# One shared block of rows for the real zeroth frequency of both batches in a Fourier and two-MoE kernel

## The chip, the cores and the metric

The kernel runs on one core of one Trainium2 chip. Time is device time in microseconds (us) for one execution of the whole program; a run reports the median of several. The engines are PE (TensorE, matrix products; PEld is its weight load), ACT (ScalarE), DVE (VectorE), POOL (GpSimd) and SP (SyncE, which here issues nearly all DMAs, one after the other). A line such as L737 is a line of the kernel as printed below.

## The reference, cut to what matters

Three layers follow one another. Only the first is touched.

```python
X = np.fft.rfft(x, axis=1)                       # x: 2 batches, 3008 positions, 256 channels
Yr = Xr @ w_r - Xi @ w_i + b_r                   # frequency mixing, 256 x 256
Yi = Xr @ w_i + Xi @ w_r + b_i
Yr, Yi = shrink(Yr), shrink(Yi)                  # sign(y) * max(|y| - 0.01, 0)
y = np.fft.irfft(Yr + 1j * Yi, n=3008, axis=1)
h = y @ w_in;  y = (h * cos(h)) @ w_out          # first MoE layer, 256 -> 2048 -> 256
h = y @ w_in2; y = (h * relu6(h + 3) / 6) @ w_out2
```

## The kernel before, in words

The transform of 3008 points is split as 47 x 64. The **first transform** (`a_part`, L562) works along the 47; of its output frequencies only k2 = 0 to 23 are made, each with a cosine row and a minus-sine row, for 64 positions n2. Its result is kept as a rounded part `zh` and a rest `zl`, with the layout (channel, pair p of two k2, half kc of the channels, four rows of 64: two per k2). For k2 = 0 the sine row is zero throughout. Batch 1's results wait in `z1` and are moved into `zh` and `zl` by `stage` (ACT and POOL) when batch 0 no longer needs the place.

For each of 12 pairs p of each of 2 batches, **mixing** (`w_mm`, L662) makes two blocks of 128 rows (two rows x 64 positions) and 512 columns (w_r and w_i), six matmuls each, and `w_split` cuts each into a rounded part and a rest (ACT, DVE). The **second transform** along the 64 (`b_mm`, L691) starts from a PSUM tile filled with the bias (`fill`) and adds six matmuls of 512 columns: two frequencies of 256 channels. `shrink_a`, `shrink_b`, `shrink_hi` and `shrink_lo` apply the threshold and split again. The **inverse** along the 64 (`v_mm`, L730) is three matmuls of 512 columns; `v_store` copies the result out of PSUM (ACT, L735) and writes it to `u_dram` in memory (SP, L737, two DMAs). Later `load_u` reads `u_dram` back with a table (L410 and L412), and `y_mm` (L421) does the inverse along the 47.

`k2_step(i)` runs these as a pipeline, 24 steps and a drain: in step i the mixing is of pair i, the second transform of pair i-1, the shrink of pair i-2, and the inverse and the store of pair i-3, all counted through both batches (so step 15 stores pair 0 of batch 1). While batch 0 is mixed, steps 0 to 7 also hold batch 1's first transform, whose data come through a ring of three buffers (`x_ring`, L542). Steps 17 to 22 (`Y_EARLY`) also hold the first six groups of `y_mm`; `load_u` of groups 0 to 3 is called at the ends of steps 14 to 17. In the same steps `cv.step` converts the MoE weights from 64-bit floats, with loads and stores of its own on SP. The order on PE, ACT and SP is the order of the program text here, and SP issues nothing behind an entry that waits. After the steps the MoE layers run, nearly all on PE.

The order inside a step that the argument needs:

```python
w_mm(b, 2 * p)                 # PE
fill(*now)                     # ACT or DVE
y_mm(...)                      # PE, steps 17 to 22
shrink_a(*late); w_split(b, 2 * p); a_part(a, 0); v_mm(*last)
shrink_hi(*late); v_store(*last); w_mm(b, 2 * p + 1)
w_split(b, 2 * p + 1); a_part(a, 1); stage(k); b_mm(*now)
```

Of the kernel before, what the change touches and what calls it, by code (L numbers as in the profile page):

```python
# [9 lines left out]
F32 = mybir.dt.float32  # L10
F32R = mybir.dt.float32r
# [3 lines left out]
AF = mybir.ActivationFunctionType  # L15
ALU = mybir.AluOpType
# [4 lines left out]
N1, N2, NSEQ = 47, 64, 3008  # L21
NB, D, DFF = 2, 256, 2048
# [29 lines left out]
Y_EARLY = range(17, 23)  # L52
FILL_DVE = range(13, 22)
LEAD = 6
OPERANDS = (1, 2, 2, 2, 2, 3)
SEVEN = (0, 2, 4, 6)
V11, V12, V22, V1, V2, V3, V4 = range(7)
# [25 lines left out]
def _tables():  # L83
    n1 = np.arange(N1)
    k2 = np.arange(NK2)
    ta = np.zeros((2, 48, NPAIR, NK2, 2))
    tg = np.zeros((2, NK2, 2, NPAIR, 2, N1))
    for i in range(NPAIR):
        for s in range(2):
            n = 64 * n1 + 2 * i + s  # L90
            c, sn = _trig(np.outer(n, k2), NSEQ)
            ta[s, :N1, i, :, 0] = c
            ta[s, :N1, i, :, 1] = -sn
            w = np.where(k2 == 0, 1.0, 2.0)[:, None] / NSEQ
            tg[s, :, 0, i, s, :] = w * c.T
            tg[s, :, 1, i, s, :] = -w * sn.T
    j = np.arange(N2)
    c, s = _trig(np.outer(j, j), N2)
    sg = np.where(j < N2 // 2, 1.0, -1.0)[None, :]
    f1 = np.zeros((2, N2, 2, N2))  # L100
    f1[0, :, 0], f1[1, :, 0] = c, s
    f1[0, :, 1], f1[1, :, 1] = -s, c
    f2 = np.zeros((2, N2, 2, N2))
    f2[0, :, 0], f2[1, :, 0] = sg * s, -sg * c
    f2[0, :, 1], f2[1, :, 1] = sg * c, sg * s
    g = np.zeros((2, N2, 2, 2, NPAIR))
    cc = c.reshape(N2, NPAIR, 2).transpose(0, 2, 1)
    ss = s.reshape(N2, NPAIR, 2).transpose(0, 2, 1)
    for z in range(2):
        g[0, :, z, 0], g[1, :, z, 0] = cc[:, z], -ss[:, z]  # L110
        g[0, :, z, 1], g[1, :, z, 1] = ss[:, z], cc[:, z]
    parts = []
    for m in (-f1, -f2, -g):
        parts += _split(m.reshape(128, 128))

    fg = np.concatenate(parts, axis=1)
    ta_rows = np.zeros((112, NPAIR * DOF))
    ta_rows[:48], ta_rows[64:] = ta.reshape(2, 48, -1)
    return (
        ta_rows.reshape(112, 4, NPAIR * 12).transpose(1, 0, 2).astype(np.float32),  # L120
        tg.reshape(ROWS, NPAIR * TP).astype(np.float32),
        np.ascontiguousarray(fg, dtype=np.float32),
    )
# [3 lines left out]
def fourier_moe_moe_kernel(ctx, tc, x, w_r, w_i, b_r, b_i, ta, tg, fg, win1, wout1, win2, wout2, out):  # L127
# [3 lines left out]
    def f32(ap):  # L131
        return ap.bitcast(F32)
# [43 lines left out]
    def pool_sub(out, x, y):  # L176
        nc.gpsimd.tensor_tensor(out, x, y, op=ALU.subtract)  # L177
# [339 lines left out]
    with ExitStack() as actx:  # L517
        apool = actx.enter_context(tc.tile_pool(name="apool", bufs=1))
        with tc.manual_schedule(engines={mybir.EngineType.PE, mybir.EngineType.SP, mybir.EngineType.Activation}):
# [54 lines left out]

            def stage(q):

                act.activation(zh[:, q], z1[:, q], AF.Copy)
                pool_sub(zl[:, q], z1[:, q], f32(zh[:, q]))

            def zero(engine, at):  # L580
                engine.memset(at, 0.0)
# [45 lines left out]
                    sp.dma_start(wst[:, k, z], w[k * 128 : (k + 1) * 128])  # L627

            def late_loads2():
                sp.dma_start(fg_raw, fg)  # L630
                for z, src in enumerate((b_r, b_i)):
                    sp.dma_start(bias[64 * z : 64 * z + 64, 0], src.partition_broadcast(64))

            def late_loads3():
                cv.add(0, range(4))

            def constants(k):
                if k < 2:
# [10 lines left out]

            def w_mm(b, k2, parts=range(2), terms=range(3)):  # L650
                p = k2 // 2
                if k2 % 2 == 0 and 0 in parts and 0 in terms:
                    ph_t[b, p] = [
                        apool.tile([128, 2, 2, D], F32R, tag=f"ph{z}", bufs=2, name=f"ph{z}_{b}_{p}") for z in range(2)
                    ]
                if 0 in parts and 0 in terms:
                    pp_t[b, k2] = h_bank(f"pp{b}_{k2}").rearrange("p (a e) -> p a e", a=2)
                pp = pp_t[b, k2]
                for kc in parts:
                    for n in terms:  # L660
                        za, wb = ((zh, wh), (zl, wh), (zh, wl))[n]
                        pe.matmul(  # L662
                            pp.rearrange("p a e -> p (a e)"),
                            lhsT=za[:, p, kc, 2 * (k2 % 2) : 2 * (k2 % 2) + 2, :].rearrange("p r n -> p (r n)"),
                            rhs=wb[:, kc, :],
                            start=(kc == 0 and n == 0),
                            stop=(kc == 1 and n == 2),
                        )

            def w_split(b, k2):  # L670
                ph, pl = (t[:, k2 % 2] for t in ph_t[b, k2 // 2])
                pp = pp_t.pop((b, k2))
                act.activation(ph, pp, AF.Copy)
                dve.tensor_tensor(pl, pp, f32(ph), op=ALU.subtract)

            def fill(b, p):

                bp_t[b, p] = bp = psum.tile([128, 2, D], F32, tag="acc0", bufs=2, name=f"bp{b}_{p}")
                rows = bias.to_broadcast([128, 2, D])
                if b * NP + p in FILL_DVE:  # L680
                    dve.tensor_copy(bp, rows)
                else:
                    act.activation(bp, rows, AF.Copy)

            def b_mm(b, p):
                bp = bp_t[b, p]
                ph, pl = ph_t.pop((b, p))
                n = 0
                for m in range(2):
                    for fi, src in ((2 * m, ph), (2 * m, pl), (2 * m + 1, ph)):  # L690
                        pe.matmul(bp, lhsT=fgr[:, fi, :], rhs=src[:, :, m, :], start=False, stop=(n == 5), skip_group_check=True)  # L691
                        n += 1

            def shrink_a(b, p):

                u_t[b, p] = persist.tile([128, 2, D], F32, tag="r", bufs=5, name=f"u{b}_{p}")
                act.activation(u_t[b, p], bp_t[b, p], AF.Relu, bias=-LAM, scale=1.0)

            def shrink_b(b, p):
                bp, u = bp_t[b, p], u_t.pop((b, p))  # L700
                dve.scalar_tensor_tensor(bp, bp, LAM, u, op0=ALU.add, op1=ALU.min)

            def shrink_sb(b, p):
# [5 lines left out]
            def shrink_hi(b, p, copy=None):  # L709
                sh = persist.tile([128, 2, D], F32R, tag="gh", bufs=4, name=f"sh{b}_{p}")  # L710
                sl = persist.tile([128, 2, D], F32R, tag="gl", bufs=5, name=f"sl{b}_{p}")
                if copy:
                    copy(sh, bp_t[b, p])
                else:
                    act.activation(sh, bp_t[b, p], AF.Copy)
                sh_t[b, p] = (sh, sl)

            def shrink_lo(b, p):
                sh, sl = sh_t[b, p]
                dve.tensor_tensor(sl, bp_t.pop((b, p)), f32(sh), op=ALU.subtract)  # L720

            def shrink_lo_sb(b, p):
                sh, sl = sh_t[b, p]
# [2 lines left out]
            def v_mm(b, p):  # L726
                vp = psum.tile([128, 2, D], F32, tag="acc1", bufs=2, name=f"vp{b}_{p}")
                sh, sl = sh_t.pop((b, p))
                for n, (fi, src) in enumerate(((4, sh), (5, sh), (4, sl))):
                    pe.matmul(vp, lhsT=fgr[:, fi, :], rhs=src, start=(n == 0), stop=(n == 2))  # L730
                vp_t[b, p] = vp

            def v_store(b, p):
                v = persist.tile([128, 2, D], F32, tag="o", bufs=4, name=f"v{b}_{p}")
                act.activation(v, vp_t.pop((b, p)), AF.Copy)  # L735
                for s in range(2):
                    sp.dma_start(  # L737
                        u_dram[b][s, 4 * p : 4 * p + 4].rearrange("(k r) i e -> (r i) k e", r=2),
                        v[64 * s : 64 * s + 64],
                    )  # L740

            def k2_step(i):
                now, late, last = (divmod(i - k, NP) for k in range(1, 4))
# [2 lines left out]
                more = i < NB * NP  # L746
                a, q = NA + i, STAGED[i : i + 2]
                if i == 0:
                    for n in range(3):
                        w_mm(0, 0, (0,), (n,))  # L750
                        w_mm(0, 1, (0,), (n,))
                    w_mm(0, 0, (1,))
                elif more:
                    w_mm(b, 2 * p)
                if i >= 1:
# [4 lines left out]
                if i >= 2:  # L760
                    shrink_a(*late)
                    cv.step(rate[0])
                    shrink_b(*late)
                w_split(b, 2 * p)
                for g, ec in early:
                    y_out(g, ec)
                if a < 2 * NA:
# [54 lines left out]
            for i in range(NB * NP):  # L822
                k2_step(i)
                if i == 0:
                    constants(2)
                if Y_EARLY[0] - 3 <= i <= Y_EARLY[0]:
                    load_u(i - Y_EARLY[0] + 3)
                if i == NB * NP - len(OPERANDS):
                    ready = operands(0)
                if i >= NB * NP - len(OPERANDS):  # L830
                    for _ in range(OPERANDS[i - NB * NP]):
                        next(ready, None)
# [544 lines left out]
```

## Time and profile before

| | |
|---|---|
| time, median of 3 runs (lowest to highest) | 1142.51 us (1142.24 to 1143.01) |
| the profiled execution's own time | 1142.83 us |
| its span, first to last instruction | 1140.8 us |
| PE busy | 1134.2 us, 99% |
| DVE, ACT, POOL busy | 78%, 75%, 76% |
| granted TensorE clock, mean | 0.999 |

The span is one execution recorded by the profiler; 2.0 us of the execution's own time lie outside it. Matmuls are pipelined, so a matmul's own length (389 ns at 512 columns) is longer than the distance from one start to the next. Where a row says "[0.40 <-PE pp L662]", the engine sat idle 0.40 us before the row and the work named released it. A landing time counts from the issue of the DMA.

### The profile page before, as it was taken

How to read it: one execution, taken by the hardware profiler on the slowest of the kernel's cores; microseconds unless marked ns; L12 is line 12 of the kernel's file. 1: busy time of each engine (PE TensorE's matmuls, PEld its weight loads, DVE VectorE, ACT ScalarE, POOL GpSimd, SP SyncE). 2: the span in 40 equal slices, each digit the busy share in tenths (PEclk: the TensorE clock that was granted, in tenths of full speed). 3: DMA queues.
4: the chain of work that ended last, by engine and by line, in shares of the span. 5: the costliest groups of instructions: out<-in, count | busy, mean ns of one | idle time of the engine just before them, and what ended most of it. 6: DMA issues, size and time to landing. Idle time of an engine off the chain costs nothing.

```text
span 1140.8 us, 16407 instructions
## 1 busy us (share of the span) xinstructions
PE 1134.2 (99%) x5285; PEld 950.3 (83%) x5285; DVE 888.7 (78%) x1302; ACT 851.0 (75%) x1627; POOL 864.1 (76%) x709
## 2 busy tenths in 40 slices
PE   9999999999999999999999999999999999999998
PEld 7888887888888887888889988888888888888897
DVE  5888876776888979887888777677787877867775
ACT  4788788777888888888888876666676676667664
POOL 3556747975997897887987987787878878777854
PEclk9999999999999999999999999999999999999999
DMA  9645968434113114012215520241231222221300
GB/s 224 192 141 173 273 183 287 153 120 154 65 59 105 36 65 139 19 60 98 75 56 193 231 94 33 65 139 32 65 107 44 90 71 64 74 94 32 100 3 33
DMA packets 73925, 120.99 MB, mean 106 GB/s; under 512 B 7904, under 2 KB 47504, under 8 KB 73328
## 3 DMA queue, kind: packets, MB, share of 16 engines
q1 hardware_dynamic: 73712, 119.80, 33.2%
q8 instruction: 42, 0.69, 0.3%
q14 instruction: 43, 0.35, 0.1%
q10 hardware_dynamic: 128, 0.15, 0.0%
HBM read 78.11 MB, written 41.81 MB: 105 GB/s over the span
## 4 chain that ended last, share of the span: by engine, by line
PE 94%; DMA 2%; DVE 1%; POOL 1%; ACT 1%; issue 1%; SPq 0%; POOLq 0%; ACTq 0%; DVEq 0%
PE acc L909 38%; PE hb L909 17%; PE ha L909 11%; PE pp L662 6%; PE hd L909 6%; PE hc L909 5%; PE part L909 5%; PE bp L691 3%; PE yp L421 2%; PE vp L730 1%; DMA x_big<-in_x_dram 1%; PE zp L562 1%; POOL gl L177 1%; DMA wst<-in_w_i_dram 1%; DVE sums L941 0%
## 5 line engine op out<-in xcount | busy, mean ns | idle before, releaser
L177 POOL TENSOR_TENSOR gl<-r,gh 128x512 fp32r<-128x512 f32 (+1 forms) x322 | 424.4, 1335 | 119.7 <-ACT gh L897 109.3
L909 PE MATMUL acc<-gh,wo 128*128 128x512 f32 (+1 forms) x1276 | 445.5, 386 | 0.0
L909 PEld LDWEIGHTS acc<-gh,wo 128*128 128x128 f32 x1276 | 239.6, 188 | 44.3
L909 PE MATMUL acc<-gl,wo 128*128 128x512 f32 (+1 forms) x638 | 246.1, 386 | 0.5 <-POOL gl L177 0.5
L909 PE MATMUL hb<-tok,wi 128*128 128x512 f32 (+1 forms) x864 | 242.1, 388 | 0.1
L897 ACT ACTIVATE gh<-r 128x512 fp32r<-128x512 f32 (+1 forms) x344 | 205.3, 617 | 4.9 <-DVE r L872 4.3
L909 PEld LDWEIGHTS hb<-tok,wi 128*128 128x128 f32 x864 | 160.1, 188 | 34.1 <-DVE hd L921 3.6
L883 ACT ACTIVATE r<-r 128x512 f32<-128x512 f32 (+1 forms) x192 | 118.7, 618 | 56.7 <-DVE r L870 56.7
L909 PE MATMUL ha<-tok,wi 128*128 128x512 f32 (+1 forms) x576 | 159.7, 385 | 0.0
L177 POOL TENSOR_TENSOR sums_lo<-sums,sums_hi 128x512 fp32r<-128x512 f32 (+1 forms) x80 | 100.7, 1277 | 62.4 <-ACT sums_hi L988 40.2
L909 PEld LDWEIGHTS acc<-gl,wo 128*128 128x128 f32 x638 | 119.8, 188 | 23.6 <-POOL gl L177 1.5
L909 PEld LDWEIGHTS ha<-tok,wi 128*128 128x128 f32 x576 | 108.0, 188 | 20.6 <-ACT yo L440 0.2
L1174 ACT ACTIVATE p<-hc 128x512 f32<-128x512 f32 (+1 forms) x96 | 56.4, 588 | 78.2 <-PE hc L909 78.0
L921 DVE TENSOR_TENSOR hd<-p,hb 128x512 f32<-128x512 f32 (+1 forms) x96 | 65.6, 683 | 62.2 <-ACT p L1174 36.3
L474 POOL TENSOR_TENSOR tok<-st,tok 128x512 fp32r<-128x512 f32 (+1 forms) x81 | 103.3, 1289 | 3.4 <-ACT tok L477 3.4
L909 PE MATMUL hc<-tok,wi 128*128 128x512 f32 (+1 forms) x288 | 80.3, 387 | 0.0
L909 PE MATMUL hd<-tok,wi 128*128 128x512 f32 (+1 forms) x288 | 79.9, 386 | 0.0
L1149 ACT ACTIVATE hb<-ha 128x512 f32<-128x512 f32 (+1 forms) x96 | 55.2, 575 | 25.8 <-PE ha L909 25.3
L921 DVE TENSOR_TENSOR hc<-p,hb 128x512 f32<-128x512 f32 (+1 forms) x96 | 65.3, 680 | 11.1 <-PE hb L909 10.2
L909 PEld LDWEIGHTS hc<-tok,wi 128*128 128x128 f32 x288 | 53.7, 188 | 11.4 <-DVE r L887 1.6
L909 PEld LDWEIGHTS hd<-tok,wi 128*128 128x128 f32 x288 | 54.1, 188 | 10.3
L474 POOL TENSOR_TENSOR st<-st 128x512 f32<-128x512 f32 (+1 forms) x44 | 56.7, 1288 | 1.2
(197 smaller groups left out, 2121.3 us busy)
## 6 DMA issues: line engine op xcount, KB each, us to landing
wo<-ws_dram SPq DMA_DIRECT2D x50, 256.0 KB, 3.2
st<-x_dram SPq DMA_DIRECT2D x18, 512.0 KB, 5.5
rawi<-in_win_dram SPq DMA_DIRECT2D x16, 512.0 KB, 4.1
rawo<-in_wout_dram SPq DMA_DIRECT2D x16, 512.0 KB, 3.8
wi<-wi_dram SPq DMA_DIRECT2D x4, 1792.0 KB, 8.5
u_dram<-v SPq DMA_DIRECT2D x48, 128.0 KB, 2.4
u_sb<-u_dram SPq DMA_DIRECT2D x16, 384.0 KB, 4.1
wo<-wo_dram SPq DMA_DIRECT2D x10, 512.0 KB, 6.5
```

The costliest lines, as they stand in the source:

```text
L177: nc.gpsimd.tensor_tensor(out, x, y, op=ALU.subtract)
L421: pe.matmul(yp[:, i * TP : (i + 1) * TP], lhsT=u_sb[g][:, i, ec * 128 : (ec + 1) * 128], rhs=tg_sb[g][:, i * TP : (i + 1) * TP], start=Tru ...
L474: (dve if jj == NJ + 1 and not ringed else nc.gpsimd).tensor_tensor(out, x, y, op=op)
L562: pe.matmul(zp[:, i * ROWS : (i + 1) * ROWS].rearrange("p (s f) -> p s f", s=2), lhsT=xt[:rows, i, kc * 128 : (kc + 1) * 128], rhs=tt[:row ...
L662: pe.matmul(pp.rearrange("p a e -> p (a e)"), lhsT=za[:, p, kc, 2 * (k2 % 2) : 2 * (k2 % 2) + 2, :].rearrange("p r n -> p (r n)"), rhs=wb[ ...
L691: pe.matmul(bp, lhsT=fgr[:, fi, :], rhs=src[:, :, m, :], start=False, stop=(n == 5), skip_group_check=True)
L883: act.activation(r, r, AF.Sin, bias=math.pi / 2, scale=1.0)
L897: act.activation(gh[:, :n], self.r[:, :n], AF.Copy)
L909: pe.matmul(h[:, :n], lhsT=w, rhs=x, start=start and j == 0, stop=stop and j == 2, skip_group_check=True)
L921: dve.tensor_tensor(h[:, :n], r[:, :n], x[:, :n], op=ALU.add)
L1149: act.activation(b[:, :n], a[:, :n], AF.Copy)
L1174: act.activation(p5[:, :n], c[:, :n], AF.Copy)
```

## The change

Both batches' zeroth frequency is real, so the second row of k2 = 0 is free. The table `ta` now has the cosine in both rows, `stage` moves only the second row of batch 1's pair 0, and so the block of pair 0, k2 = 0 of batch 1 holds batch 0 in its first 64 rows and batch 1 in its last 64. Batch 0 mixes no block for k2 = 0, and its pair 0 runs in `fill`, `b_mm`, `shrink_*`, `v_mm` and `v_store` on one frequency (256 columns). Pair 0 of batch 1 uses other tables and another bias for k2 = 0, 33 real and 31 imaginary rows per batch, so its second transform and inverse run as two sets of matmuls of 256 columns. Its `v_store` writes the zeroth rows of both batches. The new tables and the bias rows are loaded by `late_loads4` at the end of step 1 (seven DMAs on SP, two of which fill the unused sine rows of `u_dram`) and rounded by `zero_tables` (ACT) in steps 2 to 4. `load_u(0)` moves from the end of step 14 to the end of step 15, with `load_u(1)` behind it; `y_mm` stays where it was.

```diff
@@ _tables @@
             ta[s, :N1, i, :, 1] = -sn
+            ta[s, :N1, i, 0, 1] = c[:, 0]
...
+    half = NPAIR + 1
...
+    for b in range(2):
+        fz1[b, :, b, :half], fz1[b, :, b, half:] = c[:, :half], -s[:, 1:NPAIR]
+        fz2[b, :, b, :half], fz2[b, :, b, half:] = s[:, :half], c[:, 1:NPAIR]
+        gz[b, :half, :, b] = np.where(j[:half] % NPAIR, 2.0, 1.0)[:, None, None] * cc[:half]
+        gz[b, half:, :, b] = -2.0 * ss[1:NPAIR]
...
@@ stage @@
-                act.activation(zh[:, q], z1[:, q], AF.Copy)
-                pool_sub(zl[:, q], z1[:, q], f32(zh[:, q]))
+                hi, lo, z = (t[:, q, :, q == 0 :] for t in (zh, zl, z1))
+                act.activation(hi, z, AF.Copy)
+                pool_sub(lo, z, f32(hi))
...
+            def late_loads4():
+                t = persist.tile([128, 2048], F32, tag="st", bufs=1, name="zero_k2_raw")
+                zero_k2.append(persist.tile([128, 8, 128], F32R, tag="u_sb", name="zero_k2"))
+                zero_k2.extend((t[:, 768:1024], t))
+                sp.dma_start(t[:, :768], fg[:, 768:])
+                for b in range(NB):
+                    for src, o0, o1 in ((b_r, 0, NPAIR + 1), (b_i, NPAIR + 1, N2)):
+                        sp.dma_start(t[64 * b + o0 : 64 * b + o1, 768:1024], src.partition_broadcast(o1 - o0))
+                    sp.dma_start(u_dram[b][:, 1], fg[0:64, 0:D].rearrange("(s i) e -> s i e", s=2))
+
+            def zero_tables(n):
+                act.activation(zero_k2[0][:, 2 * n : 2 * n + 2].rearrange("p a b -> p (a b)"), zero_k2[2][:, 256 * n : 256 * n + 256], AF.Copy)
+
+            def columns(b, p):
+                return slice((b, p) == (0, 0), 2)
+
+            def tables(b, p):
+                if (b, p) == (1, 0):
+                    return ((slice(0, 1), zero_k2[0]), (slice(1, 2), fgr))
+                return ((columns(b, p), fgr),)
...
@@ fill @@
+                elif (b, p) == (1, 0):
+                    act.activation(bp[:, 0], zero_k2[1], AF.Copy, scale=-1.0)
+                    act.activation(bp[:, 1], bias[:, 0], AF.Copy)
                 else:
-                    act.activation(bp, rows, AF.Copy)
+                    act.activation(bp[:, columns(b, p)], rows[:, columns(b, p)], AF.Copy)
...
@@ b_mm (v_mm and the shrink functions are cut to columns and tables alike) @@
+                for cs, tab in tables(b, p):
+                    n = 0
+                    for m in range(2):
+                        for fi, src in ((2 * m, ph), (2 * m, pl), (2 * m + 1, ph)):
+                            pe.matmul(bp[:, cs], lhsT=tab[:, fi, :], rhs=src[:, cs, m, :], start=False, stop=(n == 5), skip_group_check=True)
+                            n += 1
...
@@ v_store @@
+                    if p:
+                        sp.dma_start(
+                            u_dram[b][s, 4 * p : 4 * p + 4].rearrange("(k r) i e -> (r i) k e", r=2),
+                            v[64 * s : 64 * s + 64],
+                        )
+                        continue
+                    sp.dma_start(u_dram[b][s, 2:4].rearrange("r i e -> (r i) e"), v[64 * s : 64 * s + 64, 1])
+                    for r in range(NB * b):
+                        sp.dma_start(u_dram[r][s, 0], v[64 * s + 32 * r : 64 * s + 32 * r + 32, 0])
@@ k2_step @@
                 if i == 0:
-                    for n in range(3):
-                        w_mm(0, 0, (0,), (n,))
-                        w_mm(0, 1, (0,), (n,))
-                    w_mm(0, 0, (1,))
+                    banks[0] += 1
+                    w_mm(0, 1, (0,))
...
-                w_split(b, 2 * p)
+                if i:
+                    w_split(b, 2 * p)
...
@@ the loop over the steps @@
-                if Y_EARLY[0] - 3 <= i <= Y_EARLY[0]:
-                    load_u(i - Y_EARLY[0] + 3)
+                if i == LOAD_ZERO:
+                    late_loads4()
+                if LOAD_ZERO < i < LOAD_ZERO + 4:
+                    zero_tables(i - LOAD_ZERO - 1)
+                for g in {NP + 3: (0, 1), NP + 4: (2,), NP + 5: (3,)}.get(i, ()):
+                    load_u(g)

```

## Rows read from the trace of the kernel before

**Rows 1.** The page: the chain that ended last, by engine.

```profile
PE 94%; DMA 2%; DVE 1%; POOL 1%; ACT 1%; issue 1%; SPq 0%; POOLq 0%; ACTq 0%; DVEq 0%
```

**Rows 2.** Who PE waited for, whole span: total us, times, longest us.

```profile
PE zp L562 <- DVE zl L573: 0.8, 3, 0.3
PE acc L909 <- POOL gl L177: 0.5, 2, 0.3
```

**Rows 3.** Timeline of PE in step 0: start us, us, work, count.

```profile
21.57 0.71 PE L662 MATMUL pp<-wh,zh 128*128 128x512 f32 x2
...
23.75 0.50 PE L662 MATMUL pp<-wh,zl 128*128 128x512 f32 x1
...
24.32 1.03 PE L562 MATMUL zp<-ta_ring,x_ring 96*128 96x96 f32 x8
25.14 0.48 PE L662 MATMUL pp<-wh,zh 128*128 128x512 f32 x1
```

**Rows 4.** The ring's first load: SP's timeline, and DMA issues with landing us.

```profile
17.89 0.34 SPq L542 DMA_DIRECT2D x_ring<-in_x_dram  x1
...
x_ring<-in_x_dram SPq DMA_DIRECT2D x1, 384.0 KB, 5.7
```

**Rows 5.** Timeline of PE in the first MoE layer, 512 and 448 columns.

```profile
333.44 0.84 PE L909 MATMUL ha<-tok,wi 128*128 128x512 f32 x3
334.12 0.39 PE L909 MATMUL acc<-gh,wo 128*128 128x512 f32 x1
...
627.14 0.77 PE L909 MATMUL ha<-tok,wi 128*128 128x448 f32 x3
627.75 0.36 PE L909 MATMUL acc<-gh,wo 128*128 128x448 f32 x1
```

**Rows 6.** Timeline of SP, steps 1 and 2.

```profile
32.40 0.58 SPq L542 DMA_DIRECT2D x_ring<-in_x_dram  x1
37.69 0.39 SPq L203 DMA_DIRECT2D rawo<-in_wout_dram  x1
```

**Rows 7.** Timeline of PE at the first early group of the last inverse.

```profile
116.09 1.92 PE L421 MATMUL yp<-tg_sb,u_sb 96*128 96x94 f32 x16
```

**Rows 8.** Timeline of ACT, steps 9 to 15.

```profile
82.14 0.42 ACT L302 ACTIVATE whii011h<-w 128x256 fp32r<-128x256 f32 x1
...
84.89 0.60 ACT L673 ACTIVATE ph<-pp 128x512 fp32r<-128x512 f32 x1 [0.40 <-PE pp L662]
...
104.61 0.59 ACT L735 ACTIVATE v<-vp 128x512 f32<-128x512 f32 x1
...
109.14 0.59 ACT L735 ACTIVATE v<-vp 128x512 f32<-128x512 f32 x1
```

**Rows 9.** Busy time in a stretch: PE, PEld, DVE, ACT, POOL, clock, DMA.

```profile
98.50:115.00 16.50, 16.50 (x75) 13.66 (x74) 16.21 (x24) 12.27 (x24) 11.38 (x9) 1.00 0.62 184
```

**Rows 10.** Timeline of SP, steps 14 to 16.

```profile
105.23 1.23 SPq L737 DMA_DIRECT2D u_dram<-v  x2
108.46 0.33 SPq L410 DMA_DIRECT2D u_sb<-u_dram  x1
108.86 1.24 SPq L412 DMA_DIRECT2D tg_sb<-in_tg_dram  x1
...
111.47 0.59 SPq L274 DMA_DIRECT2D wo_dram<-whio011h  x1
```

**Rows 11.** DMA issues of steps 14 to 17: count, KB, landing us.

```profile
u_dram<-v SPq DMA_DIRECT2D x2, 128.0 KB, 2.4
...
u_dram<-v SPq DMA_DIRECT2D x2, 128.0 KB, 3.1
...
u_sb<-u_dram SPq DMA_DIRECT2D x1, 384.0 KB, 3.9
...
u_sb<-u_dram SPq DMA_DIRECT2D x1, 384.0 KB, 5.9
...
tg_sb<-in_tg_dram SPq DMA_DIRECT2D x1, 141.0 KB, 4.0
```

**Rows 12.** Timeline of PE at the start of the span.

```profile
1.20 4.02 PE L618 MATMUL wp<-warm 128*128 128x512 bf16 x9 [1.20 <-DVE warm L581]
```

More of the change, by code (lines that the diff above doesn't have):

```diff
@@ L54 @@
 LEAD = 6
+LOAD_ZERO = 1
 OPERANDS = (1, 2, 2, 2, 2, 3)
@@ L111, in _tables @@
         g[0, :, z, 1], g[1, :, z, 1] = ss[:, z], cc[:, z]
+    half = NPAIR + 1
+    fz1, fz2, gz = np.zeros((2, N2, 2, N2)), np.zeros((2, N2, 2, N2)), np.zeros((2, N2, 2, 2, NPAIR))
+    for b in range(2):
[3 more added lines that the diff above has]
+        gz[b, half:, :, b] = -2.0 * ss[1:NPAIR]
     parts = []
-    for m in (-f1, -f2, -g):
+    for m in (-f1, -f2, -g, -fz1, -fz2, -gz):
         parts += _split(m.reshape(128, 128))
@@ L629, in late_loads2 @@
             def late_loads2():
-                sp.dma_start(fg_raw, fg)
+                sp.dma_start(fg_raw, fg[:, :768])
                 for z, src in enumerate((b_r, b_i)):
@@ L635, in late_loads3 @@
                 cv.add(0, range(4))
+            zero_k2 = []
+            def late_loads4():
[15 more added lines that the diff above has]
+                return ((columns(b, p), fgr),)
             def constants(k):
@@ L651, in w_mm @@
                 p = k2 // 2
-                if k2 % 2 == 0 and 0 in parts and 0 in terms:
+                if (k2 % 2 == 0 or (b, k2) == (0, 1)) and 0 in parts and 0 in terms:
                     ph_t[b, p] = [
@@ L687, in b_mm @@
                 ph, pl = ph_t.pop((b, p))
[L688 to L692, printed above, removed]
+                for cs, tab in tables(b, p):
[4 more added lines that the diff above has]
+                            n += 1
             def shrink_a(b, p):
                 u_t[b, p] = persist.tile([128, 2, D], F32, tag="r", bufs=5, name=f"u{b}_{p}")
-                act.activation(u_t[b, p], bp_t[b, p], AF.Relu, bias=-LAM, scale=1.0)
+                cs = columns(b, p)
+                act.activation(u_t[b, p][:, cs], bp_t[b, p][:, cs], AF.Relu, bias=-LAM, scale=1.0)
             def shrink_b(b, p):
-                bp, u = bp_t[b, p], u_t.pop((b, p))
+                bp, u = (t[:, columns(b, p)] for t in (bp_t[b, p], u_t.pop((b, p))))
                 dve.scalar_tensor_tensor(bp, bp, LAM, u, op0=ALU.add, op1=ALU.min)
@@ L714, in shrink_hi @@
                 else:
-                    act.activation(sh, bp_t[b, p], AF.Copy)
+                    act.activation(sh[:, columns(b, p)], bp_t[b, p][:, columns(b, p)], AF.Copy)
                 sh_t[b, p] = (sh, sl)
             def shrink_lo(b, p):
-                sh, sl = sh_t[b, p]
-                dve.tensor_tensor(sl, bp_t.pop((b, p)), f32(sh), op=ALU.subtract)
+                sh, sl, bp = (t[:, columns(b, p)] for t in (*sh_t[b, p], bp_t.pop((b, p))))
+                dve.tensor_tensor(sl, bp, f32(sh), op=ALU.subtract)
             def shrink_lo_sb(b, p):
@@ L728, in v_mm @@
                 sh, sl = sh_t.pop((b, p))
-                for n, (fi, src) in enumerate(((4, sh), (5, sh), (4, sl))):
-                    pe.matmul(vp, lhsT=fgr[:, fi, :], rhs=src, start=(n == 0), stop=(n == 2))
+                for cs, tab in tables(b, p):
+                    for n, (fi, src) in enumerate(((4, sh), (5, sh), (4, sl))):
+                        pe.matmul(vp[:, cs], lhsT=tab[:, fi, :], rhs=src[:, cs], start=(n == 0), stop=(n == 2))
                 vp_t[b, p] = vp
@@ L734, in v_store @@
                 v = persist.tile([128, 2, D], F32, tag="o", bufs=4, name=f"v{b}_{p}")
-                act.activation(v, vp_t.pop((b, p)), AF.Copy)
+                act.activation(v[:, columns(b, p)], vp_t.pop((b, p))[:, columns(b, p)], AF.Copy)
                 for s in range(2):
[L737 to L740, printed above, removed]
+                    if p:
[7 more added lines that the diff above has]
+                        sp.dma_start(u_dram[r][s, 0], v[64 * s + 32 * r : 64 * s + 32 * r + 32, 0])
             def k2_step(i):
```

## The prediction, made before the result was known

> **What bounds the kernel now.** I read the page's chain first: PE is nearly all of it [rows 1], so what counts is when PE may start each piece of work, and any matmul taken out is worth its distance to the next one. Then the waits of PE over the whole span: five times, 1.3 us in all, once the work has begun [rows 2]. DVE, ACT and POOL are busy three quarters of the time and are paid for only where PE stands still for them. The reader is to see two things in this: a removed matmul is a gain almost anywhere, and a new wait in front of PE is a loss almost anywhere, since no later idle time exists in which it could be made up. So I cost the matmuls, and then look in the timelines of PE, ACT and SP at the two places where the change puts PE closer to a DMA: step 0 and the first early group of the last inverse.
>
> **What a matmul costs.** In the dense part three matmuls of 512 columns take 0.68 us from start to start, 0.227 each; three of 448 take 0.61, 0.203 each [rows 5]. No matmul of 256 columns with these operands exists before. The line through the two sizes gives 0.13 us at 256. The bounds are 0.10, the distance between the eight passes of 96 columns (24.32 to 25.14) [rows 3], and 0.227, a half-width matmul as dear as a full one. I take 0.13, since the two nearest sizes lie on that line. The Trainium skill (TensorE: Matmul & The Clock Gate, Back-to-back issue gap) gives columns over 2.4 GHz plus 2.5 ns, so 0.109 us at 256 and 0.216 at 512; the row at 512 is 5% above it. By 0.109 the gain below would be about 1.7 instead of 1.14 us, the loads would come 0.2 earlier, and the sum would be +2.0 instead of +2.2.
>
> **What goes.** Mixing of batch 0's k2 = 0 loses six matmuls, 1.36 us of PE. But they stand in step 0, where PE meets the DMAs. Before, nine matmuls (2.04 us of work) stand between 21.57 and 24.32, where the first passes on the ring buffer start [rows 3]. After the change three stand there. They end at about 22.3 to 22.8, but the ring's first load was issued at 17.89 and lands 5.7 later, at 23.59 [rows 4]; with the weight load behind it the passes start at 23.75. That is 0.57 us won, not 1.36; at most 1.6, if the load came in time. The other three matmuls of that block then stand at 24.57, behind what they need: their second started at 23.75 before [rows 3], so they add no wait. The second transform of pair 0 is six half-width matmuls instead of six full ones: 6 x (0.227 - 0.13) = 0.58. Its inverse: 3 x 0.097 = 0.29. The split of the removed block and the halved shrink leave ACT and DVE; neither sets the end there, so I count nothing.
>
> **What is added on PE.** Pair 0 of batch 1: 12 x 0.13 against 6 x 0.227 is +0.20 in the second transform, 6 x 0.13 against 3 x 0.227 is +0.10 in the inverse. So PE arrives at the first early group 0.57 + 0.58 + 0.29 - 0.30 = 1.14 us earlier: at 114.95 instead of 116.09 [rows 7].
>
> **What is added elsewhere early.** Seven DMAs at 0.33 to 0.62 us of issue each (the prices in [rows 4, 10]) are 2.3 to 4.3 us on SP. They fall behind the ring's load of step 1, where SP issues nothing from 32.98 to 37.69 [rows 6]; cover enough, and what stands behind them (the next ring load and a weight load) is for two steps later. Without that cover the ring's loads would slip by that much. The three roundings on ACT cost 0.42 each at this size [rows 8]. The first may wait for its DMA, by an estimate from the ring's 5.7 us of landing under 2 us; behind it stand a fill and a shrink whose result PE takes a step later. I count nothing, and up to 1 us upward. The smaller `stage` of pair 0 gains POOL and ACT nothing that PE waits for.
>
> **The moved load.** This decides. `load_u(0)` now reads rows that `v_store` of step 15 writes, so it must wait for that store to land, and SP issues nothing behind it while it waits. Queued there are `load_u(1)`, the weight load of step 16 and the next store; PE needs none of them before it needs group 0. How long the chain from store to data is, step 14 shows, which has the same chain: ACT copies the result at 104.61, the store's two DMAs are issued from 105.23 on, in 1.23 us, the load at 108.46, the table's at 108.86 [rows 8, 10]. The second store DMA started at about 105.84 and landed 2.4 later [rows 11], at 108.24; the load followed 0.2 us after. It landed after 3.9 us, the table after 4.0: data at about 112.9, 8.3 us after ACT began its copy. PE asks at 116.09, so 3.2 us were spare. One step later, and with four more DMAs, they aren't.
>
> The working for step 15. ACT's copy stood at 109.14 [rows 8]. ACT last waited for PE at 84.89 [rows 8] and from 98.50 to 115.00 DVE is busy 16.21 of 16.50 us [rows 9], so ACT and DVE run there on what they had earlier: they come forward by what PE had won by step 10, 0.57 + 0.58 + 0.29 = 1.44, and lose about 0.1 (0 to 0.25) to the bias now filled in two pieces. The copy starts at 107.8. The first store DMA goes out 0.62 later as in step 14, at 108.4. Six DMAs stand there instead of two. Before, one took 0.61 with 128 pieces of 1 KB; these have 32 or 64 pieces, and the short loads cost 0.33 [rows 4, 10]: I take 0.5 (0.33 to 0.62). The sixth starts at 110.9 and lands 2.4 to 3.1 later [rows 11]; with 2.4, 113.3. The two weight stores behind it (0.59 and less each, [rows 10]) go out in that time. `load_u(0)` is issued at 113.5, its table at 113.9. The u load took 3.9, but 5.9 right behind weight stores [rows 11]; these now stand a microsecond ahead, so I take 4.7: landing at 118.2, the table with it. PE starts `y_mm` at 118.3, 0.1 for the weight load. It has stood still from 114.95, 3.3 us, and is 2.2 us later than before, at a point from which nothing can be made up.
>
> Bounds: with 0.33 per DMA, 2.4 and 3.9 landing, 1.4 of lead, the data are there at 117.0, +0.9. With 0.62, a landing of 3.1, 5.9 and only 0.9 of lead, at 121.3, +5.2.
>
> **The sum.** The profiled execution took 1142.83, its span 1140.8 and 2.0 around it; plus 2.2 is 1145.0. The median of the runs shown is 0.3 below the profiled one, so 1144.7. A measurement of this kernel can tell about 0.2%, 2.3 us, from no change: the sum lies on the edge of that.
>
> **Rivals.** *The wait is hidden* (not slower): if the moved load's data were there at 114.95, the matmul sum would stand alone, 1.14 us faster, 1141.4. It needs the chain from ACT's copy to the data to be 7.1 us with six store DMAs; it was 8.3 with two [rows 8, 10, 11]. Between this and the forecast lie mild waits, under +0.9. Together 14%.
>
> *The whole of the matmuls is won*: the ring lands in time, 256 columns cost 0.10 and there is no wait: 1.6 + 0.76 + 0.38 + 0.16 + 0.08 = 3.0 faster, 1139.5. Against it stands the landing at 23.59 [rows 4]. 5% for all that is over 0.2% faster.
>
> *The wait is longer*: the store's pieces land late behind weight stores, or the issue costs the full 0.62: +3.5 to +5.2, 1146.0 to 1147.7. For it speaks the one u load that took 5.9. 12%.
>
> *PE is slow after the hole*: the nine opening matmuls take 4.02 us, at most 0.45 apart instead of 0.227 [rows 12]. Nine such after the hole cost up to another 2.0 us: 1146.7. It decides only if a hole of 3.3 us suffices; PE nowhere stands still so long before, so no row shows it. The Trainium skill (TensorE: Matmul & The Clock Gate, Part 1) says that an engine left idle is set to half its clock and given it back only after activity; the granted clock here is 1.00 wherever I looked [rows 9]. 7%.
>
> *The forecast*, a hole of 2 to 4.5 us, +0.9 to +3.5: 62%, half of it on either side of the 2.3 us.
>
> **How the numbers follow.** Slower by over 0.2%: 31 + 12 + 7 = 50%. Within 0.2%: 31 + 14 = 45%. Faster by over 0.2%: 5%. The likeliest is 1144.7. The range is 1142.4 to 1147.4: it leaves out the case with all gains and most of the hidden one below, and the end of the long waits above.
>
> **What the changed profile would show.** PE's timeline: passes on the ring at about 23.75; half-width matmuls 0.13 apart; at step 17 an idle stretch of 2 to 4.5 us before the yp group at L421, released by a DMA of u_sb or tg_sb, with SP waiting for u_dram before the load. The rest of the timeline shifted by a constant. I am wrong if the yp group starts without a wait, if the store DMAs go out well before 108, if the waits of PE late in the MoE layers shrink by as much as the hole costs, or if the granted clock falls below 1.00 behind it.

## The result and the profile after

| | before | changed |
|---|---|---|
| time, median of 6 runs (lowest to highest) | 1142.38 us (1140.39 to 1143.01) | 1150.21 us (1148.59 to 1154.18) |
| ratio, 95% interval | | 1.0073 [1.0063, 1.0083] |
| the profiled execution's own time, its span | 1142.83, 1140.8 | 1149.49, 1147.4 |
| mean granted TensorE clock | 0.999 | 0.996 |

The changed kernel is 7.8 us slower, where 2.2 were forecast; 1150.21 lies above the range. The page's chain (share by engine) has less PE than in [rows 1] and more DMA and DVE, and the waits of PE (total us, times, longest) name three places that [rows 2] doesn't have:

```profile
PE 88%; DMA 4%; DVE 3%; ACT 2%; issue 1%; POOL 1%; SPq 1%; POOLq 0%; ACTq 0%; DVEq 0%
```

```profile
PE yp L430 <- DMA tg_sb<-in_tg_dram: 3.2, 1, 3.2
PE pp L695 <- DVE ph L707: 1.5, 1, 1.5
...
PE zp L571 <- DMA x_ring<-in_x_dram: 0.5, 1, 0.5
```

The timeline of PE of the changed kernel (start us, us, work, count, wait in front) shows where they stand:

```profile
20.66 0.48 PE L695 MATMUL pp<-wh,zh 128*128 128x512 f32 x1
...
22.57 1.10 PE L571 MATMUL zp<-ta_ring,x_ring 96*128 96x96 f32 x8 [0.46 <-DMA x_ring<-in_x_dram]
...
29.60 0.96 PE L728 MATMUL bp<-ph,fgr 128*128 128x256 f32 x6
30.39 0.40 PE L695 MATMUL pp<-wh,zh 128*128 128x512 f32 x1
...
47.27 0.50 PE L695 MATMUL pp<-wh,zh 128*128 128x512 f32 x1 [1.53 <-DVE ph L707]
...
115.25 0.39 PE L695 MATMUL pp<-wl,zh 128*128 128x512 f32 x1
118.87 3.70 PE L430 MATMUL yp<-tg_sb,u_sb 96*128 96x94 f32 x16 [3.23 <-DMA tg_sb<-in_tg_dram]
122.28 1.20 PE L769 MATMUL vp<-sh,fgr 128*128 128x512 f32 x2
```

The last three rows are the wait of step 17 and what follows it. The yp group that took 1.92 us in [rows 7] takes 3.70 here. The busy times by stretch (PE, PEld, DVE, ACT, POOL, granted clock, DMA share) say why:

```profile
110.50:117.80 7.30, 5.14 (x23) 3.94 (x21) 7.23 (x11) 4.29 (x9) 5.57 (x5) 1.00 0.72 207
117.90:124.60 6.70, 5.73 (x22) 5.28 (x23) 2.16 (x5) 2.05 (x4) 2.35 (x4) 0.50 0.97 265
124.80:130.00 5.20, 5.20 (x33) 4.53 (x32) 3.70 (x8) 2.89 (x6) 0.00 (x0) 1.00 0.79 213
```

PE stood still from 115.6 and the clock granted to it was 0.50, that is 1.2 instead of 2.4 GHz, from 117.9 to 124.6.

To see what each place costs, I set the starts of the second transforms (24 groups of `bp`, one a step) of both kernels side by side, changed minus before. The changed kernel's profiled execution is 0.9 us ahead before anything of the change has run (20.66 against 21.57 in [rows 3]); that belongs to the opening loads and differs from execution to execution. Then:

| place | ahead (-) or behind (+), us |
|---|---|
| before step 0 | -0.9 |
| bp of step 1 | -1.68 |
| bp of step 2 | -2.33 |
| bp of step 3 | -2.68 |
| bp of step 4 | -0.86 |
| bp of step 16 | -0.60 |
| yp of step 17 | +2.78 |
| bp of step 17 | +5.60 |
| end of the span | +6.6 |

So the gains came nearly as forecast (1.8 us by step 3, where 1.44 were forecast), were eaten in step 4 (1.8), and step 17 cost 3.4 by its wait and 2.8 more behind it. The chain of step 4 is new. SP's timeline, the landing of the weight load, and the timelines of ACT and DVE in the changed kernel:

```profile
34.80 0.25 SPq L656 DMA_DIRECT2D zero_k_raw<-in_b_i_dram  x1
35.10 0.59 SPq L657 DMA_DIRECT2D u_dram<-in_fg_dram  x1
36.03 0.41 SPq L212 DMA_DIRECT2D rawo<-in_wout_dram  x1
```

```profile
rawo<-in_wout_dram SPq DMA_DIRECT2D x1, 512.0 KB, 7.2
```

```profile
43.33 0.67 ACT L215 ACTIVATE cvao<-rawo 128x512 f32<-128x512 f32 x1 [2.68 <-DMA rawo<-in_wout_dram]
...
44.42 0.58 ACT L706 ACTIVATE ph<-pp 128x512 fp32r<-128x512 f32 x1
```

```profile
46.54 0.68 DVE L707 TENSOR_TENSOR ph<-pp,ph 128x512 fp32r<-128x512 f32 x1
```

The same load in the kernel before:

```profile
rawo<-in_wout_dram SPq DMA_DIRECT2D x1, 512.0 KB, 3.8
```

The weight load behind the seven new DMAs lands 7.2 us after its issue; before, the same load took 3.8. ACT reaches `cvao` with nothing else to do and waits 2.68 us, with PE's next split queued behind it; DVE finishes that split at 47.2, and PE, which had come to it early, has lost its lead.

### The profile page after: what moved, and what is told of

Same layout as the page of the kernel before. It is cut to its first block, busy times and chain, and to the rows that moved or that the text cites. A ratio compares the mean times of both kernels' runs of the same rounds, so it can differ in the third digit from the quotient of the medians.

```text
span 1147.4 us, 16427 instructions
## 1 busy us (share of the span) xinstructions
PE 1135.4 (99%) x5288; PEld 951.3 (83%) x5288; DVE 885.2 (77%) x1301; ACT 850.9 (74%) x1630; POOL 863.4 (75%) x709
## 4 chain that ended last, share of the span: by engine, by line
PE 88%; DMA 4%; DVE 3%; ACT 2%; issue 1%; POOL 1%; SPq 1%; POOLq 0%; ACTq 0%; DVEq 0%
PE acc L956 37%; PE hb L956 16%; PE ha L956 10%; PE hd L956 5%; PE hc L956 5%; PE part L956 5%; PE pp L695 3%; PE yp L430 3%; PE bp L728 2%; DMA x_big<-in_x_dram 1%; PE vp L769 1%; DMA rawi<-in_win_dram 1%; DMA rawo<-in_wout_dram 1%; PE zp L571 1%; DVE sums L988 1%
## 5 line engine op out<-in xcount | busy, mean ns | idle before, releaser
L934 DVE TENSOR_TENSOR r<-r,hb 128x512 f32<-128x512 f32 (+1 forms) x48 | 32.4, 674 | 33.0 <-ACT r L930 32.9
```

The source lines that it names most:

```text
L934: dve.tensor_tensor(r, r, self.h[:, : self.n], op=ALU.mult)
```

## Experiments

My theory after the profile: three causes add up, namely the weight load held up in step 4, the wait in step 17, and the half clock behind that wait. Ratios are to runs of the kernel before on the same chip.

### The wait filled with matmuls (e1_filled)

```diff
                 for g, ec in early:
-                    y_mm(g, ec, h_bank(f"yp{g}_{ec}"))
+                    yp = h_bank(f"yp{g}_{ec}")
+                    for _ in range(16 * (i == Y_EARLY[0] and ec == 0)):
+                        pe.matmul(yp, lhsT=fgr[:, 0, :], rhs=wh[:, 0, :], start=True, stop=True)
+                    y_mm(g, ec, yp)
```

> The changed kernel, with 16 matmuls whose result is thrown away (512 columns, 0.227 us each) in front of the first early yp group, where PE stands still for 3.2 us. The wait for the data stays. Theory (the profile's half clock behind the hole costs 2.9 us): the granted clock stays at 1.00, the 16 yp matmuls take 1.9 us instead of 3.7, and the kernel takes 2.5 to 3 us less than the changed one, about 1147.4. Rival (the yp group and what follows are slow because their data or ports are busy with the loads that land there): the yp group takes 3.7 us as before and the time stays at 1150.

1146.19 us, ratio 1.0043 [1.0027, 1.0059]. PE's timeline and the clock by stretch:

```profile
114.39 3.79 PE L803 MATMUL yp<-wh,fgr 128*128 128x512 f32 x16
118.02 1.92 PE L430 MATMUL yp<-tg_sb,u_sb 96*128 96x94 f32 x16
```

```profile
117.90:124.60 6.70, 6.70 (x39) 5.81 (x38) 3.33 (x7) 3.71 (x7) 1.44 (x2) 1.00 1.05 296
```

The filler takes as long as the wait did, the group begins as late, and it runs in 1.92 us at a clock of 1.00 while the DMAs are as busy as before (share 1.05). So the slow group was the clock, not data or ports. From step 16 to the end of step 17 this kernel loses 3.6 us, the changed one 6.2: the clock cost 2.6 in the profiles. The medians differ by 4.0, more than that one stretch explains.

### The first early group at the end of its step (e2_y_end)

```diff
+                first = early if i == Y_EARLY[0] else []
+                early = [] if first else early
 ...
                 if i >= 1:
                     b_mm(*now)
+                for g, ec in first:
+                    y_mm(g, ec, h_bank(f"yp{g}_{ec}"))
+                for g, ec in first:
+                    y_out(g, ec)
```

> The changed kernel, with the first early yp group at the end of step 17 instead of its start, behind 3.4 us of matmuls that need nothing of it. Theory (hole and clock are one cause, the load moved by a step): the yp group starts with a wait under 0.6 us, the granted clock stays at 1.00, and the time falls by the hole and the clock, 3.2 + 2.9, to about 1144. Rival (the store and load of step 15 hold up SP so that the next loads are late too): PE waits at a later group or in front of the MoE layers, and the time stays above 1147.

1144.27 us, ratio 1.0018 [1.0006, 1.0031]: as the theory said. No wait for DMA is left in step 17, and 6 us of the loss are gone. Its profile also shows the wait of step 4 alone, 1.8 us here, and behind it:

```profile
47.38 0.79 PE L695 MATMUL pp<-wh,zh 128*128 128x512 f32 x1 [1.77 <-DVE ph L707]
47.97 0.63 PE L695 MATMUL pp<-wh,zl 128*128 128x512 f32 x1
48.39 0.63 PE L695 MATMUL pp<-wl,zh 128*128 128x512 f32 x1
```

```profile
47.40:50.70 3.30, 3.30 (x10) 2.72 (x10) 3.19 (x5) 2.02 (x5) 2.66 (x3) 0.50 0.00 0
```

The matmuls start 0.43 apart instead of 0.227, at a granted clock of 0.50. In this execution the stall of step 4 cost 3.6 us instead of 1.8.

### What holds up the weight load (e3_rows16, e5_bias16, e6_fill16)

e5 has the first edit, e6 the second, e3 both:

```diff
-                    for src, o0, o1 in ((b_r, 0, NPAIR + 1), (b_i, NPAIR + 1, N2)):
+                    for src, o0, o1 in ((b_r, 0, NPAIR), (b_i, NPAIR, N2)):
 ...
-                    sp.dma_start(u_dram[b][:, 1], fg[0:64, 0:D].rearrange("(s i) e -> s i e", s=2))
+                    for s in range(2):
+                        sp.dma_start(u_dram[b][s, 1], fg[32 * s : 32 * s + 32, 0:D])
```

> The changed kernel, with the bias rows of the shared block loaded as 32 and 32 rows instead of 33 and 31, and the unused rows of u_dram written in four DMAs of 32 rows instead of two of 2 x 32 (one bias row in each half is that of the imaginary part: that part of the computation is changed). Bytes are the same, two DMAs more. Theory (a DMA whose row count shares no factor with the 16 engines runs on few of them, and the weight load behind waits for the slowest): the rawo load of step 2 lands in 4 to 5 us instead of 7.2, ACT doesn't wait 2.7 us for it in step 4, and PE does not stand still 1.5 us at the pp of step 4. Rival (the bytes or the seven issues on SP delay it): the landing stays at 7 us. The time falls by 0 to 1.8 us, since PE then only comes earlier to the hole of step 17.

> The changed kernel with the bias rows as 32 and 32 instead of 33 and 31 (one row in each half has the other part's bias), the two DMAs of 2 x 32 rows into u_dram left as they are. Theory (the loads of 31 rows run on one engine and hold up what is behind them there): the rawo load of step 2 lands in 4 to 5.5 us and PE's wait in step 4 is under 0.6 us. Rival (the two writes of 2 x 32 rows on two engines hold it up): it still lands in 6.5 us or more. Only landing and wait are read, not the time.

> The changed kernel with the writes into the unused rows of u_dram as four DMAs of 32 rows, the bias loads left at 33 and 31 rows. Theory (the 31 rows): the rawo load still lands in 6.5 us or more and PE still waits over 1 us in step 4. Rival (the 2 x 32 writes): it lands in 4 to 5.5 us. Only landing and wait are read, not the time.

Landing of the first rawo load in e3, in e5, and in e6 (there from the chain of work, start us, us):

```profile
rawo<-in_wout_dram SPq DMA_DIRECT2D x1, 512.0 KB, 4.3
```

```profile
rawo<-in_wout_dram SPq DMA_DIRECT2D x1, 512.0 KB, 6.8
```

```profile
38.86 0.49 SPq L658
...
39.45 4.24 DMA rawo<-in_wout_dram
```

My theory named the wrong one of the new DMAs. e5 and e3 differ in the writes into `u_dram` alone: with the two writes of 2 x 32 rows the load lands in 6.8 us, with four of 32 rows in 4.3. e6 and e3 differ in the bias loads alone (31 and 33 rows against 32) and land alike, in 4.2 and 4.3. So the two writes of 2 x 32 rows hold it up. One reservation belongs to e6: with two more DMAs SP issues the load 6.5 us after the first of the new DMAs, instead of 4.7 in the changed kernel, so part of its short landing may be time in which the queue emptied. Between e5 and e3 the issue differs by 0.3 us only (4.8 and 5.0 after the first new DMA), the landing by 2.5. The Trainium skill (DMA: Bandwidth & Descriptors, Why a DMA increments its semaphore by 16 and not by 1) says that a DMA runs on as many engines, up to 16, as divide the slowest dimension of both sides: two for 2 x 32 rows, 16 for 32 rows, one for 31 rows. The runs agree for the writes; of the 31-row loads, by that rule the worse, none shows a cost.

The wait of PE in step 4, 1.5 us in the changed kernel, is in e3, in e6 and in e5:

```profile
PE pp L696 <- DVE ph L708: 0.4, 1, 0.4
```

```profile
PE pp L696 <- DVE ph L708: 0.3, 1, 0.3
```

```profile
PE pp L695 <- DVE ph L707: 1.2, 1, 1.2
```

Counted from the first of the new DMAs, ACT starts on the load 12.0 us later in the changed kernel, 11.7 in e5, 10.8 in e6 and 9.4 in e3. How much of the 1.8 us the cut writes give back in their place these runs don't say: e3 and e6 came to step 4 with a smaller lead (0.1 and 1.0 us instead of 2.7), and all three have the wait of step 17 and its half clock in their time. e3 took 1147.77 us, ratio 1.0056 [1.0038, 1.0075], e5 1149.52 and e6 1149.37 (one time each).

### The store with two DMAs instead of six (e7_two_stores)

```diff
-                    for r in range(NB * b):
+                    for r in range(0):
                         sp.dma_start(u_dram[r][s, 0], v[64 * s + 32 * r : 64 * s + 32 * r + 32, 0])
 ...
+                if i == 8:
+                    for b in range(NB):
+                        for s in range(2):
+                            sp.dma_start(u_dram[b][s, 0], fg[32 * s : 32 * s + 32, 0:D])
```

> The changed kernel without the four added store DMAs of step 15: the zeroth rows of both batches are not stored (those rows of u_dram are filled with table values in step 8, so that part of the result is left out). The loads stay at step 15. Theory (the four issues on SP, 0.53 us each, stand between the store and the load): the load of group 0 is issued 2.1 us earlier after ACT's copy, PE's wait in step 17 falls from 3.2 to about 1.1 us, the clock stays at 1.00, and the time falls by 5, to about 1145. Rival (the data of step 15 are late because the DMAs that land there share the engines): the wait stays above 2.5 us.

SP and PE in the changed kernel, then in this one:

```profile
109.20 0.48 SPq L782 DMA_DIRECT2D u_dram<-v  x1
...
113.52 0.32 SPq L419 DMA_DIRECT2D u_sb<-u_dram  x1
```

```profile
107.72 1.11 SPq L782 DMA_DIRECT2D u_dram<-v  x2
...
110.14 0.33 SPq L419 DMA_DIRECT2D u_sb<-u_dram  x1
```

```profile
116.23 1.99 PE L430 MATMUL yp<-tg_sb,u_sb 96*128 96x94 f32 x16 [2.07 <-DMA tg_sb<-in_tg_dram]
```

The load follows the first store DMA by 2.4 instead of 4.3 us, so the four issues cost 1.9, as supposed. But the data then took 6.1 us from the issue of the load instead of 5.3, and the wait fell to 2.07, not 1.1. The clock did not stay at 1.00 either: it is 0.50 from 118.5 to 121.9, half as long as in the changed kernel. 1148.15 us, ratio 1.0060 [1.0042, 1.0079], in runs from 1144.77 to 1151.51; the profiled one is the fastest, so this profile does not tell what the median lost. Half of the expectation failed: even the store of before leaves a wait once the load stands a step later.

### The loads alone in the kernel before (e8_loads_alone)

```diff
+                if i == 1:
+                    late_loads4()
+                if 1 < i < 5:
+                    zero_tables(i - 2)
```

> The kernel before, with nothing of the change but the seven DMAs at the end of step 1 and the three roundings on ACT (their results are not used; the two writes go to another place in memory). Theory: the rawo load of step 2 lands in about 7 instead of 3.8 us, ACT waits for it in step 4, PE stands still there for 1.5 to 3.5 us, and the kernel is 1.5 to 3.5 us slower, at about 1144 to 1146. Rival (the wait in step 4 comes of PE being ahead there): PE does not wait, and the time is that of before.

1142.91 us, ratio 1.0009 [1.0000, 1.0018]. The load lands in 7.0 us, ACT starts `cvao` at 44.13 after waiting 2.2, but PE waits only 0.3 us there:

```profile
PE pp L685 <- DVE ph L697: 0.3, 1, 0.3
```

Both sides are half right. The landing is late whatever else changes; how much PE pays depends on when it comes to the split. This execution was 0.63 us ahead, by its opening, and lost 0.54 of it by step 4 and 0.64 by step 5; the changed kernel was 2.68 ahead and lost 1.82 in step 4. The lead alone does not give the price: e7's execution, which has the same loads, came 3.30 us ahead and lost 0.94. That the late landing took away what the removed matmuls had given is shown by the next run, where the load lands early and the lead stays.

### All three causes mended (e4_mended, e9_split_loads)

e4 has the edit of e2; the bias rows laid out beside the tables in the `fg` array, so that one DMA of 128 rows brings both; the writes into `u_dram` as four DMAs in step 8; the roundings a step later:

```diff
-                sp.dma_start(t[:, :768], fg[:, 768:])
+                sp.dma_start(t[:, :1024], fg[:, 768:])
 ...
+                if i == 8:
+                    sine_rows()
```

> The changed kernel with both mends: the yp group of step 17 at its end, the bias rows of the shared block carried in the table's array so that tables and bias come in one DMA of 128 rows, the unused rows of u_dram written in step 8 by four DMAs of 32 rows, and the roundings one step later. Theory (three causes explain the whole loss): no wait in step 4, none or under 0.6 us in step 17, clock 1.00: 0.8 to 1.4 us faster than the kernel before, 1141.0 to 1141.6. Rival (something else of the change costs time too, in the MoE layers for example): at or above the kernel before.

1141.50 us (11 runs), ratio 1.0000 [0.9991, 1.0009]. The three losses are gone: `rawo` lands in 3.6 us, PE waits for no DMA or split in steps 4 to 16 (its lead is 1.59 us in step 3 and 1.58 in step 4), and between the opening and the last microseconds the clock is 1.00 throughout. The gain of 0.8 to 1.4 us is not shown: the time lies where it was expected, but the kernel before had a median of 1142.29 beside it, and the interval holds both no gain and one of 1 us. The lead of 1.15 us at step 16 also shrinks to 0.12 in step 18. ACT's timeline shows one more wait:

```profile
122.29 0.66 ACT L215 ACTIVATE cvao<-rawo 128x512 f32<-128x512 f32 x1 [2.71 <-DMA rawo<-in_wout_dram]
```

The weight load of step 16 now stands behind both groups' loads. So e9 takes the tables of groups 0 and 1 out of that queue and moves the rows of group 1:

```diff
-                for g in {NP + 3: (0, 1), NP + 4: (2,), NP + 5: (3,)}.get(i, ()):
-                    load_u(g)
+                for g, parts in {NP + 2: ((0, "t"), (1, "t")), NP + 3: ((0, "u"),), NP + 4: ((1, "u"), (2, "ut")), NP + 5: ((3, "ut"),)}.get(i, ()):
+                    load_u(g, parts)
```

> The first mended kernel, with the loads of the early groups spread: the tables of groups 0 and 1 are loaded at the end of step 14 (they depend on nothing), the rows of group 0 at the end of step 15, those of group 1 one step later, so that the weight load of step 16 has one load in front of it instead of four. In the first mended kernel ACT waited 2.7 us for that weight load and PE lost 1.0 us in steps 17 and 18. Theory (that queue costs the 1.0 us): PE keeps its lead of 1.2 us through step 18 and the kernel is about 1.2 us faster than the one before, 1141. Rival (the rows of group 1 now come too late for step 18): PE waits there, and the time is that of before or above.

1140.71 us against 1141.35 before (11 and 21 runs), ratio 0.9995 [0.9987, 1.0004]. Of the waits of PE once the opening is past, one of 0.2 us is left in the whole span:

```profile
PE zp L574 <- DMA x_ring<-in_x_dram: 0.2, 1, 0.2
PE acc L968 <- POOL gl L186: 0.2, 1, 0.2
```

The lead falls by 0.6 us in steps 17 and 18 instead of 1.0, so by these two profiles that queue cost 0.4 us, and the rest is open. This version has the lowest median, but its gain of 0.6 us can't be told from none; the expected 1.2 lie inside the interval too.

### All early groups late (e10_all_late)

As e9, with the first edit below in place of e2's, so that all six groups stand at the ends of their steps. Its output is not that of the reference, for a reason that was not found, so only the order of its work is read.

```diff
-                first = early if i == Y_EARLY[0] else []
-                early = [] if first else early
+                first, early = early, []
```

> As the one with the spread loads, and with all six early groups at the ends of their steps, so that group 1 has 5 us more. Theory: no wait of PE for DMA in steps 17 to 22, the lead of 1.2 us stays, 1.0 to 1.4 us faster than the kernel before, 1140.6 to 1141. Rival (copying the groups out at the end of a step collides with the bias fill and the thresholds on ACT): PE waits for DVE or ACT in those steps, and the time is that of before or above.

1141.37 us, ratio 0.9995 [0.9986, 1.0004]. No wait for DMA in steps 17 to 22, but PE waits 0.5 us for ACT's bias fill (`bp`, L723), and about 0.8 us of lead go behind step 22: the rival's collision, at the end of the row of groups. (By the starts of `bp` alone it would be 2.5 us, but in steps 17 to 22 a group of 1.7 us that stood in front of `bp` stands behind it here.)

## Why the prediction was wrong

**What held.** The half-width matmul: six take 0.79 us (29.60 to 30.39), 0.132 each, and in pair 0 of batch 1 0.12; 0.13 was taken. By that the 0.109 of the Trainium skill was too low. Step 0: the passes on the ring waited 0.46 us for their load, and PE won 0.8 there, not 1.36; 0.57 was forecast. The second transform and the inverse gave 0.65 and 0.35 (0.58 and 0.29). Pair 0 of batch 1 cost 0.10 and 0.05, half of what was put down.

**What held of the moved load.** This was the deciding term, and its ends came out almost to the tenth: six store DMAs at 0.53 us each (0.5 taken), the load issued at 113.52 (113.5), the group begun at 118.87 (118.3), a wait of 3.23 (3.3). In part that is luck. The first store DMA went out at 109.20, not at 108.4, because ACT and DVE had come forward by less; the stores then landed in 1.6 us instead of 2.4, and the two errors cancel. And PE came to the group at 115.64, not at 114.95, though this execution had a head start of 0.9 us that is not of the change: the lead had gone in step 4. e7 shows that the added issues are 1.9 us of the chain, and e2 that the wait is what stood behind the loss.

**The step that failed first: "I count nothing" for the seven DMAs.** I named SP's free time as their cover and looked only at issue. SP was indeed free. But a DMA is not done when it is issued, and the weight load behind these landed in 7.2 instead of 3.8 us. I had called it "for two steps later"; in truth ACT takes it in order in step 4, with PE's split behind it. e5 and e3 show which DMAs did it, e8 that the loads alone hold up the weight load, and e4 that the lead stays when it lands early. Mis-sized: 0, with up to 1 us upward; measured 1.8 us in the profiled execution.

**The rival that came true.** The half clock behind the wait had 7% and a price of up to 2.0 us. It came, at 2.6 to 2.8 us, and e1 shows that it is the clock. The price was too low because I took nine slow matmuls from the opening for the whole of it; the stretch at 0.50 held the yp group, the inverse and half a block of mixing. Its chance was too low: the row said only that PE never stands still for long before the change, and I read the missing row as evidence against. The Trainium skill (TensorE: Matmul & The Clock Gate, Part 1) has the rule that an idle PE drops to half its clock; every run with a wait of 3 us agrees (0.50 in the changed kernel, e3, e5 and e6), and shorter waits are in the last section.

**What stays open.** The profiled execution won 1.8 us by step 3, lost 1.8 in step 4, 0.3 up to step 16, 3.4 and 2.8 in step 17 and 1.0 from there to the end: 7.5 us in all, of which the head start of 0.9 leaves the 6.6 of the table. The medians differ by 7.8. The 1.0 us at the end, in the MoE layers, drifts up and down, between 5.3 and 6.4 us behind, and the runs show nothing of the change in it: from step 24 to the end e8, with the MoE layers of before, falls back by 1.3 us, and e9 comes forward by 0.8. How much the clock cost in the median is open too. The single executions of the changed kernel have a mean clock between 0.993 and 0.999, and the longest, 1154.18 us, has the lowest; but the one with 0.999 took 1149.18 us, about as long as the profiled one with 0.996. By an estimate from these means the clock cost it about 1 us and the profiled one about 4.6, so something else took the difference there; that execution has no profile.

## What to carry to other kernels

A DMA that is free to issue is not free: look at what lands behind it, in what blocks of rows it is written, and which in-order engine takes the delayed data with other work queued behind. When a load is moved behind a store, walk the whole chain, copy, issues, landing, load, landing, against the slack of the next step, and put the matmuls that need it last in their step. A wait of PE costs more than its length when the clock falls behind it, which here happened with waits from 1 us upward, though not with all, so price such a wait with a stretch at half clock, or fill it.

## What the runs showed of the hardware

The length of a wait of PE did not settle by itself whether the granted clock fell to 0.50. A wait of 1.77 us in step 4 was followed by 3.3 us at 0.50 in e2; waits of 1.53 in the same place (the changed kernel), 1.4 (e1) and 1.2 (e5) were followed by none. In step 0 a wait of 0.99 us was followed by 3.3 us at 0.50 in e3, one of 1.13 by none in e6. In step 17 waits of 3.2 and 2.07 us were followed by stretches at 0.50 of about 6.7 us (the changed kernel, the last 1.0 us of the wait included) and 3.4 (e7). The fall can come late: in e7 PE had worked for 2.2 us again when the clock fell, in e3's step 0 for 1.1. These stretches may be one source of the wide scatter of the kernels with waits (5.6 us in the changed one, 2.6 in the one before); by the mean clocks above they are not the only one.

The opening, which waits for the first loads, differs between executions: in kernels that are the same up to there the first matmul of mixing starts between 20.00 us (e1) and 21.61 (e6). In step 0 the wait for the ring's load, 0.1 to 1.1 us, and in e3 the half clock come on top. The second transform of step 1 then starts between 2.66 us ahead of the kernel before (e1) and 0.92 behind it (e3); the change's own gain of about 0.8 us is in both. So a single profile says little of gains under 2 us unless places inside it are compared.
